# The opening and the first group put on a written time line, with wide exponentials and folds on two engines

## The chip, the cores and the metric

The kernel runs on one core of one Trainium2 chip. Its engines are TensorE (PE, matrix multiplications), VectorE (DVE), ScalarE (ACT), GpSimd (POOL) and SyncE (SP, which issues most DMA transfers). Each works through its own queue in order and waits on semaphores for the others; DMA transfers move data between the chip's memory (DRAM) and the on-chip memory (SBUF), and TensorE writes its results to accumulator banks (PSUM). The metric is the device time of one execution in microseconds (us), as the median of several runs. Profiles are of one execution each.

## The reference: what is computed

An attention block without the usual score matrix, followed by a Fourier mixing block. Input: `q`, `k`, `v` of shape (8 batches, 8 heads, 576 tokens, 64), and weights `w_ch1` (512 x 2048) and `w_ch2` (2048 x 512).

```python
q_s = softmax(q, axis=-1)            # over the 64 of a head
k_s = softmax(k, axis=2)             # over the 576 tokens
kv  = einsum('bhsd,bhse->bhde', k_s, v)
x   = einsum('bhsd,bhde->bhse', q_s, kv)   # then heads side by side: (8, 576, 512)
u   = x + real(fft(fft(x, axis=1), axis=2))
un  = (u - mean) / sqrt(var + 1e-6)  # over the 512
out = u + relu(un @ w_ch1) @ w_ch2
```

Both softmaxes subtract a maximum first and add 1e-9 to the sum.

## The kernel before

**Tiles and groups.** Tokens are rows of 128 partitions. A batch has four "own" tiles of 128 tokens, called by (c, u) with c and u in 0 and 1; the few tokens that these leave over are gathered for two batches at a time in one "shared" tile (rows 0, 32, 64 and 96 of it come from elsewhere in DRAM than the 31 rows after each). The eight batches and the shared rows make eight groups of 512 tokens that go through the two large matmuls: first "up" (with `w_ch1` and relu), then "down" (with `w_ch2`).

**Stages.** For a batch, the keys (four tiles of 128 x 576, two heads each) get a maximum, an exponential with its sum (L634), a transpose on TensorE (L652, L660), and the product with the values (L677); the result is scaled by the reciprocal (L689) into `kvr`. A query tile gets a maximum by head (L731), eight exponentials with one head each (L737), a sum and reciprocal (L742 to L744), a product with it (L750), a transpose (L758), and the product with `kvr` (L811). The Fourier transforms are done by folding: sums and differences of tiles and of mirrored columns (L866, L872, L881, L887, L888; all on VectorE for batch 0, divided between VectorE and GpSimd for later ones), then matmuls with tables (the "blocks", L922 and L925) and again (the "mixes", L959 and L962), whose results are added to x (L992, L993). The norm takes statistics (L1013), a root, and scales (L1034 for group 0), then transposes (L1048) into `unT` (L1056).

**The first group.** The weights come as 64-bit words and are converted block by block ("convert", L379 to L385: two operations on ScalarE, two on VectorE, an exact integer addition on GpSimd). Group 0 goes through plain matmuls with the converted blocks: L1122 (up, 16 steps of four matmuls) and L1131 (down, 64 matmuls). Meanwhile sums and differences of the weight blocks ("combine", L391 to L401) are made and stored to DRAM (L431 to L437), because the later groups use a Strassen scheme (L1186 and after). The attention of batch 1 is worked in between.

**What sets the order.** From the second group on, steps carry times and are sorted by them inside `tc.manual_schedule`: each engine's queue has exactly this order. The opening and the first group are outside it: their order on each engine follows a scheduler, which may exchange instructions, and small instructions that copy a value onto itself or combine two with an "and" of zero ("gates": L576, L290, L306, L310, L312) hold back what should come later. While batch 0's folds run, two pairs of junk matmuls (L234) keep TensorE busy.

The order of DMA issues is that of the queue which issues them. Transfers use eight completion semaphores in turn, and a transfer waits for the earlier user of its own. The shared tile of queries is loaded by ScalarE's queue in four pieces of 32 rows each, and a fifth transfer of 4 rows, from SyncE, then writes over the first row of each piece (`t_rows`, L330 and L331). The outputs of the same rows go out in pieces of 15 and 16 rows (`shared`).

## Time and profile before

| | |
|---|---|
| median of 3 runs | 1095.81 us (1094.34 to 1096.25) |
| the profiled execution | 1096.12 us |
| its span, first to last instruction | 1094.3 us |
| TensorE busy over the span | 1057.3 us (97%) |
| VectorE, ScalarE, GpSimd busy | 662.2, 413.8, 484.8 us |
| first matmul of group 0's up phase | 61.90 us from the span's start |
| first matmul of its down phase | 116.91 us |
| first matmul of the second group | 195.62 us |

How to read it: busy time on TensorE is an upper bound of its work, since matmuls overlap. A line of the timeline gives the start, the duration of the merged instructions, the engine, the line of the program, the operation, what it writes and reads, how many instructions are merged, and in brackets how long the engine sat idle before them and what released it. Because merged matmuls overlap with the next ones, the time from one start to the next is the better measure. In the chain that ended last, 82% of the span are TensorE's.

### The profile page before, as it was taken

The numbers are of one execution on the slowest core, as the hardware profiler recorded it, in microseconds if no ns is written. First come the engines' busy times: TensorE is split into PE (matmuls) and PEld (weight loads), VectorE is DVE, ScalarE is ACT, GpSimd is POOL, SyncE is SP. The second block draws the span as 40 slices with busy tenths as digits, with TensorE's granted clock in tenths as the row PEclk, the third lists the DMA queues.
The fourth block names the chain that finished last, engine by engine and source line by source line (L and its number), as shares of the span: only waits on it lengthen the run. The fifth ranks groups of instructions, "written<-read, shape, count | busy, mean of one in ns | idle before, by whom it ended". The sixth has DMA issues, their size and how long they took to land.

```text
span 1094.3 us, 16985 instructions
## 1 busy us (share of the span) xinstructions
PE 1057.3 (97%) x6336; PEld 918.2 (84%) x6336; DVE 662.2 (61%) x1304; ACT 413.8 (38%) x1001; POOL 484.8 (44%) x410
## 2 busy tenths in 40 slices
PE   5799989999999999999999999999999999999997
PEld 4644545888888899889998999889988998899896
DVE  6784796566545775757654775687547743562251
ACT  6685433552135314442344224521552132131200
POOL 1065572227323536255533742464435353554343
PEclk9999989999999999999999999999999999999999
DMA  9555787546997457555766576557644574576463
GB/s 306 189 199 187 268 283 243 171 146 217 315 325 260 175 192 261 193 187 193 245 233 209 175 246 208 206 201 243 236 164 155 197 254 165 204 243 213 168 242 124
DMA packets 114914, 236.42 MB, mean 216 GB/s; under 512 B 24320, under 2 KB 76288, under 8 KB 104208
## 3 DMA queue, kind: packets, MB, share of 16 engines
q1 hardware_dynamic: 113032, 234.29, 63.3%
q10 hardware_dynamic: 1800, 1.05, 0.3%
q8 instruction: 50, 0.82, 0.3%
q14 instruction: 32, 0.26, 0.1%
HBM read 200.18 MB, written 39.32 MB: 219 GB/s over the span
## 4 chain that ended last, share of the span: by engine, by line
PE 82%; DVE 3%; ACT 1%; issue 1%; POOL 1%; POOLq 0%; DVEq 0%; ACTq 0%
PE bb L1186 15%; PE bb L1312 10%; PE ba L1186 9%; PE bc L1186 9%; PE bc L1312 6%; PE ba L1312 6%; PE bb L1282 4%; PE acc L677 2%; PE acc L811 2%; PE bb L1397 2%; PE bc L1131 2%; PE acc L922 2%; PE acc L925 2%; PE acc L959 1%; PE bc L1397 1%; PE ba L1397 1%
## 5 line engine op out<-in xcount | busy, mean ns | idle before, releaser
L1186 PE MATMUL bb<-unT,big 128*128 128x256 f32 x768 | 184.1, 380 | 0.0
L391 POOL TENSOR_TENSOR big<-big 128x512 f32<-128x512 f32 (+1 forms) x38 | 46.3, 1219 | 278.6 <-ACT big L1198 277.8
L1186 PEld LDWEIGHTS bb<-unT,big 128*128 128x128 f32 x768 | 142.9, 190 | 18.8 <-DVE unT L1062 0.4
L1198 ACT ACTIVATE big<-big 128x512 f32<-128x512 f32 x96 | 60.4, 630 | 199.7 <-DVE big L1197 199.5
L1156 DVE TENSOR_TENSOR u<-bb,s 128x512 f32<-128x512 f32 x66 | 45.6, 691 | 130.2 <-PE bb L1186 114.3
L1186 PE MATMUL ba<-unT,big 128*128 128x256 f32 x512 | 123.9, 380 | 0.2 <-ACT unT L1056 0.2
L1186 PE MATMUL bc<-unT,big 128*128 128x256 f32 x512 | 123.9, 380 | 0.0
L1312 PE MATMUL bb<-big 128*128 128x128 f32 x848 | 105.2, 276 | 2.2 <-DVE u L1319 2.2
L1186 PEld LDWEIGHTS ba<-unT,big 128*128 128x128 f32 x512 | 94.7, 190 | 12.3 <-ACT unT L1056 0.5
L1186 PEld LDWEIGHTS bc<-unT,big 128*128 128x128 f32 x512 | 94.5, 190 | 12.1 <-DVE big L1197 0.9
L1312 PEld LDWEIGHTS bb<-big 128*128 128x128 f32 x848 | 99.7, 192 | 2.9 <-DVE u L1319 2.9
L1258 DVE TENSOR_TENSOR big<-big 128x512 f32<-128x512 f32 x92 | 83.0, 946 | 5.9 <-POOL big L392 3.4
L1262 POOL TENSOR_TENSOR x<-x,big 128x512 f32<-128x512 f32 x52 | 68.0, 1318 | 28.0 <-ACT big L1289 14.8
L1312 PE MATMUL ba<-big 128*128 128x128 f32 x640 | 79.6, 275 | 0.0
L1312 PEld LDWEIGHTS ba<-big 128*128 128x128 f32 x640 | 76.4, 192 | 1.2
L1258 POOL TENSOR_TENSOR big<-big 128x512 f32<-128x512 f32 x26 | 41.2, 1593 | 74.1 <-DVE big L1258 64.0
L737 ACT ACTIVATE q<-q,qm 128x64 f32<-128x64 f32 x240 | 64.6, 338 | 20.6 <-DVE qm L731 15.2
L1319 DVE TENSOR_TENSOR u<-bb,s 128x256 f32<-128x256 f32 x40 | 16.9, 423 | 70.5 <-PE bb L1312 61.8
L1282 PE MATMUL bb<-big 128*128 128x256 f32 x256 | 58.7, 381 | 0.0
L1197 DVE TENSOR_TENSOR big<-bc,u 128x512 f32<-128x512 f32 x64 | 44.0, 687 | 23.7 <-PE bc L1186 22.6
L1282 PEld LDWEIGHTS bb<-big 128*128 128x128 f32 x256 | 48.3, 190 | 7.9 <-DVE big L1197 1.1
L1312 PE MATMUL bc<-big 128*128 128x128 f32 x416 | 51.5, 275 | 0.0
(280 smaller groups left out, 2039.9 us busy)
## 6 DMA issues: line engine op xcount, KB each, us to landing
big<-w2d SPq DMA_DIRECT2D x67, 1024.0 KB, 4.9
big<-w1s SPq DMA_DIRECT2D x64, 896.0 KB, 4.9
big<-w2s SPq DMA_DIRECT2D x16, 1024.0 KB, 6.6
big<-in_w_dram SPq DMA_DIRECT2D x21, 512.0 KB, 5.9
w2d<-big SPq DMA_DIRECT2D x42, 256.0 KB, 6.1
q<-in_q_dram SPq DMA_DIRECT2D x27, 256.0 KB, 6.6
k<-in_kT_dram SPq DMA_DIRECT2D x24, 288.0 KB, 5.2
v<-in_v_dram SPq DMA_DIRECT2D x24, 256.0 KB, 5.2
```

Source lines behind the costliest of these rows:

```text
L391: e1.tensor_tensor(out=to(4), in0=at(2), in1=at(3), op=ALU.add)
L677: nc.tensor.matmul(pk, lhsT=ks[:, c, :], rhs=v[:, c, :], start=(c == 0), stop=(c == NC - 1))
L737: nc.scalar.activation(q[:, h, :], q[:, h, :], ACT.Exp, bias=m[:, h:h + 1])
L1156: plus = lambda t: V.tensor_tensor(out=temp(t), in0=box["bb"][:], in1=box["s1"][:], op=ALU.add)
L1186: nc.tensor.matmul(bank()[:, i, :], lhsT=w[:, WA_AT[m], k * P:(k + 1) * P], rhs=self.unT[g][:, B_AT[m], k, :], start=first and i == 0 and ...
L1197: steps = [(0, lambda: V.tensor_tensor(out=hp(i), in0=bank()[:], in1=u()[:], op=ALU.add)), (0.8, lambda: nc.scalar.activation(hp(i), hp(i) ...
L1198: (0.8, lambda: nc.scalar.activation(hp(i), hp(i), ACT.Relu))]
L1258: e.tensor_tensor(out=to(o), in0=to(x), in1=to(y), op=op)
L1262: G.tensor_tensor(out=x, in0=x, in1=tile(m), op=ALU.add)
L1282: nc.tensor.matmul(box[name][:, i, :], lhsT=h[p][:, A_AT[m], i * P:(i + 1) * P], rhs=self.stream[n][:, p, :], start=p == 0 and (m != 1 or ...
L1312: nc.tensor.matmul(box[place[n]][:, i, :], lhsT=own(m)(A_AT[n])[:, f, :], rhs=w[:, r // 2, r % 2 * P:r % 2 * P + P], start=first and f == ...
L1397: nc.tensor.matmul(bank()[:, i, :], lhsT=h[p][:, A_AT[m], i * P:(i + 1) * P], rhs=w[:, p, :], start=first and i == 0 and p == 0, stop=p == ...
```

## The change

The opening and the first group move into `tc.manual_schedule`. The opening's order is a table of step names with times (OPENING); a step is an operation of one engine or a few. In detail:

- Loads: the four key tiles of batch 0 are issued first, then values and queries in turn. The shared query rows come in four transfers of 31 rows and one of 4 rows, all on ScalarE's queue (`loads_first`).
- Queries of batch 0: GpSimd subtracts the maximum from the whole tile ("less"), and ScalarE takes one exponential of 512 columns ("exp"). For the own tiles the sum over a head comes from a matmul with a matrix of ones (`ones`) before the product with `kvr`, and its reciprocal scales the product.
- Keys of batches 0 and 1: the last 64 tokens of all four tiles are transposed together into `fifth`; the four products with the values share one bank, one reciprocal serves four tiles, and two operations of 64 x 4 x 64 scale.
- Folds of batch 0: the sums are GpSimd's, the differences VectorE's; GpSimd also takes the shared rows' folds and one of the two additions after each mix of batch 0.
- Norm of group 0: two of the four scalings are ScalarE's. The table of the root is loaded ahead ("roots").
- The junk matmuls and the gates are removed.
- Conversions and combinations are lists of timed steps. Combinations of the first layer come in the up phase, those of the second in the down phase (before, both came in the down phase). The attention of batch 1, its folds, mixes and norm get times in the group too.

```diff
+OPENING = """
+4.60 t max, 5.20 k00 max, 5.35 t less, 6.00 k00 exp, 6.20 k01 max, 6.76 t exp, 6.95 k00 turn, 7.20 k02 max,
+7.26 k01 exp, 7.87 t inverse, 8.02 k00 four, 8.21 k01 turn, 8.52 k02 exp, 8.72 k03 max, 9.28 k01 four,
...
+12.76 k00 kv, 13.09 B max, 13.59 t join, 13.69 A exp, 13.81 k01 kv, 14.29 B less, 14.71 A turn, 14.90 C max,
...
+23.56 k11 turn, 23.71 k10 four, 24.15 D out, 24.21 k11 four, 24.28 tokens0, 24.77 tokens2, 25.38 columns0,
+25.39 tokens3, 25.98 tokens1, 26.01 columns2, 26.37 columns3, 26.85 by3, 27.08 columns1, 27.20 c0 hi,
+27.21 by2, 27.69 again2, 27.85 c0 lo, 27.99 again3, 28.49 by0, 28.59 b2 times, 28.80 c1 hi, 28.85 by1,
...
+43.31 normal10, 43.67 normal11, 43.81 k1 scale1, 43.96 turn10, 44.22 laid00, 44.72 laid10, 44.87 turn11,
+45.62 laid11"""
...
-    def warm(self, t, n):
-
-        junk = self.turned()
-        for _ in range(n):
-            self.nc.tensor.matmul(junk[:, 0:2, :], lhsT=self.ident[:], rhs=t, start=True, stop=True)
...
-        last = self.t_rows(b, tail, nc.scalar)
-        t = self.small.tile([P, 1], F32, tag="root", name="root", bufs=1)
-        nc.scalar.activation(t[:], self.eps[:], ACT.Exp)
...
+        def shared():
+            flat = self.q.rearrange("b s n -> (b s) n")
+            for i in range(4):
+                a = i * S // 2 + P
+                nc.scalar.dma_start(tail[i * Q + 1:(i + 1) * Q], flat[a + 1:a + Q])
+            nc.scalar.dma_start(tail[0:P:Q], flat[0:2 * S:S // 2])
...
+        order = [shared, table, *(lambda r=r: keys(r) for r in range(NR)), lambda: values(0), lambda: queries(0),
+                 lambda: values(2), lambda: queries(1), self.tables, *(lambda r=r: second(r) for r in range(NR)),
+                 *(lambda i=i: fetch(i) for i in range(11))]
+        return [(i / 100, step) for i, step in enumerate(order)]
...
+        def last():
+            box["last"] = self.turned()
+            for r in range(NR):
+                nc.tensor.transpose(box["last"][:, r, :], ks[r][:, S - P:], self.ident[:])
+
+        def fifth():
+            copy(self.fifth[64:], box["last"][64:])
...
+        def scale(h):
+            s = slice(64 * h, 64 * h + 64)
+            V.tensor_tensor(out=self.kvr[b][s, :, s], in0=box["kv"][s, :, s],
+                            in1=rec[s].unsqueeze(2).to_broadcast([64, NR, 64]), op=ALU.mult)
...
+        def less():
+            m = live[it].pop()[:].unsqueeze(2).to_broadcast([P, H, DH])
+            nc.gpsimd.tensor_tensor(out=heads(), in0=heads(), in1=m, op=ALU.add)
+
+        def exp():
+            q = live[it][0]
+            nc.scalar.activation(q, q, ACT.Exp)
...
+            if b == 0:
+                n = {(0, 0): "bb", (1, 1): "bc", (0, 1): "ba", (1, 0): "bb"}[c, u]
+                t = self.ps.tile([P, 512], F32, tag=n, name=n)
+                box.append(t)
+                for r in range(NR):
+                    nc.tensor.matmul(t[:, 0:H], lhsT=qT[:, r, :], rhs=self.ones[:, r, :], start=r == 0, stop=r == NR - 1)
...
         def tokens_folded(some):
             for i in some:
-                e, op = ((V if b == 0 else G), ALU.add) if i < 2 else (V, ALU.subtract)
+                e, op = (G, ALU.add) if i < 2 else (V, ALU.subtract)
...
         def columns_folded(some):
             for i in some:
-                e, op = ((V if b == 0 else G), ALU.add) if i < 2 else (V, ALU.subtract)
+                e, op = (G, ALU.add) if i < 2 else (V, ALU.subtract)
                 t = eo[i]
                 e.tensor_tensor(out=t[:, 1:HD], in0=t[:, 1:HD], in1=t[:, D - 1:HD:-1], op=op)
-                if b == 0 and i > 1:
-                    self.warm(t[:, 0:HD], 2)
...
-            if self.turns == 2:
-
-                t = self.small.tile([P, 1], F32, tag="root", name="root", bufs=1)
-                nc.scalar.activation(t[:], sn[:, 0:1], ACT.Sqrt, scale=0.0)
...
+    first, second, both = 46.5, 56, 77
+    steps = blk.opening(fetch, converted)
+    up, down = blk.plain(0, lambda: blk.unT[0])
     for f in range(NF):
...
+        steps += at(first + 3.45 * f, up[f])
+    for i in range(2, 2 * NF - 6):
+        steps += at(first - 0.4 + 2 * (i - 2) if i < NF else first + 26 + 3 * (i - NF), converted(i))
+    for p, dt in enumerate((15, 20, 25, 35.5, 39, 42.5, 46, 50)):
+        steps += at(first + dt, combined(0, p))
+    t = first + second
+    for i, some in enumerate(down):
+        steps += at(t + 1.2 * i, some)
...
+    for p, dt in zip((3, 0, 1, 7, 2, 4, 5, 6), (28, 31, 34, 37, 46, 53, 58, 63)):
+        steps += at(t + dt, combined(1, p))
...
+        at_q = t - 14 + 6 * i
...
+        steps += at(at_q + 9, blk.q_turn(it)) + at(at_q + 13.5, blk.q_times_kv(it))
+    steps += at(t + 11, blk.t_times_kv(1)) + at(t + 19, blk.folded(1))
...
+    steps += at(t + 51, blk.norm(1)) + at(t, blk.ahead(2))
```

The names of the table: "t" is the shared query tile, "k02" key tile 2 of batch 0, A to D the own query tiles (0, 0), (1, 1), (0, 1), (1, 0), "tokens", "columns", "by" and "again" the four stages of the folds, "b2" a block, "m0" a mix, "c0" a conversion.

## The prediction

> **What bounds the kernel now.** I read the page's forty slices first, then the engines' busy time in stretches of 10 us, then the timeline of single engines where a stretch was thin. The slices:
>
> ```profile
> PE   5799989999999999999999999999999999999997
> PEclk9999989999999999999999999999999999999999
> ```
>
> TensorE is full from about 200 us on. What can be won lies in the first eight slices. From the built programs, the last 3018 matmuls, 989 VectorE and 365 SyncE instructions stand in one order in both kernels, so whatever moves the first matmul of the next group moves the end by the same amount. The timeline of TensorE gives the marks:
>
> ```profile
> 61.90 0.67 PE L1122 MATMUL ba<-unT,big 128*128 128x512 f32 x1 [1.12 <-ACT unT L1056]
> ...
> 143.07 2.08 PE L811 MATMUL acc<-kvr,qT 128*128 128x128 f32 x8 [4.01 <-ACT qT L768]
> 144.94 1.06 PE L758 MATMUL tr<-ident,spare 128*128 128x128 f32 x4
> 145.79 3.47 PE L1131 MATMUL ba<-big 128*128 128x512 f32 x4
> ...
> 195.62 1.99 PE L1186 MATMUL ba<-unT,big 128*128 128x256 f32 x8 [0.24 <-ACT unT L1056]
> ```
>
> The opening lasts 61.90 us, the first group 133.72 us. In the group TensorE idles 4.01 us, and then L811 takes 1.87 us from start to start where it takes 0.89 elsewhere, L758 0.85 for 0.44, four L1131 3.31 for 1.72: 2.98 us more at a low clock. With the 0.24 before L1186 that is 7.2 us; the other 126.5 are work. The low clock is in the stretches too:
>
> ```profile
> 130.00:140.00 10.00, 9.06 (x39) 5.13 (x37) 7.92 (x18) 3.33 (x8) 7.03 (x9) 1.00 0.75 293
> 140.00:150.00 10.00, 6.93 (x19) 4.50 (x20) 9.97 (x13) 6.36 (x12) 7.21 (x7) 0.66 0.68 247
> ```
>
> (window, TensorE, its weight loads, VectorE, ScalarE, GpSimd, then the clock.) How the opening begins, on VectorE, then on the two DMA queues:
>
> ```profile
> 4.13 0.75 DVE L628 TENSOR_REDUCE km<-big 128x1 f32<-128x576 f32 x1 [4.13 <-DMA big<-in_kT_dram]
> ...
> 7.87 0.75 DVE L628 TENSOR_REDUCE km<-big 128x1 f32<-128x576 f32 x1 [1.91 <-DMA big<-in_kT_dram]
> ```
>
> ```profile
> 0.75 1.90 ACTq L330 DMA_DIRECT2D big<-in_q_dram  x4
> ```
>
> ```profile
> 7.55 0.69 SPq L331 DMA_DIRECT2D big<-in_q_dram  x1
> ```
>
> The DMA view of the first 30 us has ScalarE's queue and the rates:
>
> ```profile
> GB/s 0 0 110 270 340 296 329 304 303 350 369 352 178 256 306 311 330 284 374 370 387 391 389 365 359 344 326 331 332 333 330 306 339 345 352 350 350 347 350 348
> ...
> q10 hardware_dynamic: 192, 0.26, 3.0%
> ```
>
> VectorE starts when key tile 0 lands, 3.4 us after its issue. The four loads of 32 shared query rows are all in by 7.55, where L331, which writes over them, is let go. Their 192 packets are 4 x (32 rows + 16).
>
> **What the skill says.** In "DMA: Bandwidth & Descriptors", section "Why a DMA increments its semaphore by 16 and not by 1", the Trainium skill says that a transfer is split over the largest count of engines, up to 16, that divides its outermost size, and gives 127 partitions as an example of one engine, the lowest. The 16 packets beside each 32 rows agree with 16 engines; no transfer of a prime count of rows is in this trace. "SBUF — State Buffer", section "Who interferes with whom", says that a VectorE instruction with two SBUF inputs and a GpSimd one that reads SBUF hold the shared ports in turn. This trace agrees:
>
> ```profile
> 156.04 3.12 POOL L866 TENSOR_TENSOR eo<-x 128x512 f32<-128x512 f32 x2
> ```
>
> ```profile
> 156.28 1.75 DVE L866 TENSOR_TENSOR eo<-x 128x512 f32<-128x512 f32 x1
> 157.96 1.35 DVE L849 TENSOR_TENSOR eo<-eo 128x128 f32<-128x128 f32 x1
> ```
>
> Alone the same VectorE instructions take 0.68 (at 154.26) and 0.29 (at 26.97). "TensorE: Matmul & The Clock Gate", section "Part 1: The HAM clock gate", halves the clock after an idle window of about 3.4 us; the 4.01 above, with 6 us of doubled times after it, agrees.
>
> **The change, part by part.** The new names are those of the table OPENING.
>
> *The shared query load.* Four loads of 32 rows, overwritten by a fifth, become four of 31 and a fifth of 4 rows, all from ScalarE; the fifth waits until the first has landed. "t max", which needs all five, is now VectorE's first instruction: the key maxima, then every exponential, wait behind it. 31 is prime. If the rule holds, 4 x 31 x 2048 B = 254 KB go through one engine, which also carries a sixteenth of what SyncE has under way: four key tiles (73.7 KB), the first values (41.0), the first queries (32.8). That is 401 KB. A sixteenth of 350 to 389 GB/s is 21.9 to 24.3 GB/s, so 16.5 to 18.3 us. Key tile 0 shows what lies around moving: 3.4 us less its 18.4 KB (0.84) = 2.55. Issued at 0.75, the rows land at 19.8 to 21.6; I take 20.5. Ends: 13.8 if the queue were served first (254 KB at 24.3 = 10.5), 23.5 if the second values come between. SyncE suffers as well: its loads wait for semaphores in turn with those loads, so values and queries come late; the second queries, near 25, are needed only at about 31. If the rows spread as before, they land near 8.4: 7.55, and the fifth after that.
>
> *From that landing (L) to the first up matmul.* Five rows of the sum:
> - "t max" 0.60 and key maximum 0 0.70; ScalarE then has four key exponentials (0.78), a wide one for t (about 0.6, from 0.68 for 576 columns) and copies (0.5); the last transposes at the cold 1.05, and the copy "k0 fifth" 0.55: first keys-times-values at L + 8.7.
> - Four of these at 1.22 and a turn at 0.44, two scales of 0.45, "t kv" 0.9 and hand-overs: L + 16.0. One shared reciprocal and two scales stand for four and eight (0.29 each). Of the own tiles' 8 x 0.25 us of exponentials, one of 0.6 each remains; ScalarE isn't what this stretch waits for.
> - Four own tiles: 0.89 each, and the new head sums by matmul: eight passes of 8 columns. No row shows such a pass. Below, nothing; above, 0.86 by the skill's weight-load price (page above, "LDWEIGHTS": 107 ns for 128 columns). I take 0.7. With a turn: 6.8, L + 22.8.
> - The folds. VectorE alone took from 32.47 to 38.35 for the part the sine blocks need. Divided, GpSimd's 1.25 + 0.65 + 1.25 + 0.65 alternate with VectorE's 0.53 + 0.53 + 0.27 + 0.27 (0.08 to 0.15 of each is not port time), 5.4, and then by3, by2, again2 and again3 take 1.5; with the last product's copy 7.2: L + 30.0. Below, about 5 if the ports didn't clash.
> - TensorE has nothing for about 6 us of that (L234's warming matmuls are removed), so the five blocks cost 4.9 + 3.0 at the low clock (0 to 3.5), copies 0.7: first mix at L + 38.6. Mix to up took 61.90 - 46.99 = 14.9; 1.3 of it goes with L973's table load (1.28), now earlier, 1.1 with two of four scalings moved to ScalarE: 12.5. Up at L + 51.1.
>
> With 20.5 this is 71.6, 9.7 us later than now.
>
> *Weights and group 0.* Conversions are the same work, one each 2 to 3 us. The first layer's combinations move into the up phase, where GpSimd was free from 103 to 114 us: 8 x 1.44 us there beside 24 additions of 1.25, 42 of TensorE's 55. Their stores pass the fetches of later weights on SyncE, and a combination that overwrites a stored block waits for the landing (4.8 us in the DMA table), with VectorE's and GpSimd's conversions queued behind it: some 4 us, three times, which the 13 free ones hide. Without that cover up would wait for a conversion, but these run a dozen us ahead. Gates (L576, L290, L310, L306) go. So the 4.01 + 2.98 of before go, in which ScalarE stood behind L576 and combinations. I leave 2.5 us (0 to 7) for new waits: the first query turn has 1.6 us of room behind VectorE. Group: 129.0, 4.7 less. Loads for the next groups are only reordered, under a full TensorE: nothing.
>
> Sum: +9.7 - 4.7 = +5.0. Span 1099.3; the profiled execution's 1096.12 becomes 1101.1, and the median of the runs lies 0.3 below it: about 1100.5.
>
> **The rivals.**
> *Spread after all* (the other side). The loads use all engines, L = 8.4: up at 59.5, 2.4 earlier, and the group's 4.7: 1089. For it: 16 engines at 32 rows, and OPENING sets "t max" at 4.60. Against: the code loads 32 rows and overwrites one elsewhere, and splits the same 31 rows in 15 + 16 for the output. It decides where L is below 61.9 + 4.7 - 51.1 = 15.5.
> *Half late.* One engine, but its rows get more than an even share, or the folds and the clock cost their lower ends: L near 15, or 66 for up: 1096, no change.
> *The plan as written.* Up at 46.5, 15.4 earlier, with the group 20: 1076. Against: it needs ports that don't clash and rows at 4.60.
> *Group 0 stalls.* VectorE, held behind a combination that waits for stores, delays the first query turn; 4 us idle and 3 of low clock come back: 1108.
>
> **How the numbers follow.** Main case 0.62 (1094 to 1107), spread 0.15, half late 0.15, plan 0.03, stall 0.05. The landing's ends alone give -7 to +3, the unknown prices -6 to +1. The range 1086 to 1108 leaves out the plan, half of spread's lower part and the worst. Within 0.2% (2.2 us) is about what a measurement can't tell from none. Slower: 0.54 of the main case, stall, 0.02 of half late, 0.61. Same: 0.14. Faster: spread, plan, and the rest, 0.25.
>
> **What would show it.** ScalarE's queue: 128 rows + 4 x 1 + 4 = 136 packets if narrow, 208 if spread. VectorE's first instruction near 20.5, released by a DMA; the DMA rate below 200 GB/s before it. Folds with doubled VectorE times; blocks near 1.9 us; up near 71.6; group 0 at 129. The prediction falls if "t max" starts before 15.

## The result, and the profile after

The changed kernel takes 1119.78 us (median; 1118.97 to 1120.43), the kernel before, on the same chip, 1095.07: a ratio of 1.0225, 95% interval 1.0208 to 1.0243. The forecast was 1100.5 and its range ended at 1108. The sign was right, the size was not: 24.7 us where 5 were forecast.

The profiled execution of the changed kernel took 1118.97 us, its span 1117.2, against 1096.12 and 1094.3 before. The two marks on TensorE's timeline divide the difference of 22.9:

| stretch | before | forecast | after |
|---|---|---|---|
| opening, to the first up product | 61.90 | 71.6 | 70.93 |
| group 0, to the second group's first product | 133.72 | 129.0 | 147.82 |
| second group's first product at | 195.62 | 200.6 | 218.75 |

The opening came out 0.7 us from the forecast. Group 0 was to gain 4.7 us and lost 14.1: the whole miss is there.

The opening first. VectorE's first instruction, in VectorE's timeline (start, duration, operation; in brackets the idle time before it and what ended it):

```profile
19.82 0.69 DVE L798 TENSOR_REDUCE qm<-big 128x8 f32<-128x512 f32 x1 [19.82 <-DMA big<-in_q_dram]
```

And the DMA view of the first 30 us, the rates in forty equal slices, then ScalarE's queue:

```profile
GB/s 0 0 150 248 325 358 370 120 51 250 389 75 26 26 25 23 27 190 179 384 167 25 111 371 385 53 25 52 150 418 437 395 391 404 342 387 357 371 378 351
...
q10 hardware_dynamic: 136, 0.26, 2.3%
```

136 packets is the count forecast for one engine a load. The stretches at 23 to 27 GB/s are that one engine, with nothing else under way: SyncE's queue waits for these rows before it issues the next values and queries (5.9, 3.0 and 3.1 us; the first of these waits covers 9 to 11.8 us). Before, the same forty slices fall under 170 GB/s only at the very start. The sign "below 200 GB/s before it" came only in part: 17 of the 26 slices before 19.5 us are below.

Now group 0, in TensorE's timeline:

```profile
70.93 5.37 PE L1156 MATMUL ba<-unT,big 128*128 128x512 f32 x8 [0.77 <-ACT unT L1110]
...
129.94 1.09 PE L815 MATMUL tr<-ident,q 128*128 128x128 f32 x4 [5.58 <-DVE q L787]
...
173.66 1.82 PE L994 MATMUL acc<-ft,eo 128*128 128x144 f32 x4 [6.36 <-DVE eo L963]
```

(With a gap in the records of a few tenths, the idle times before these two are 5.75 and 6.5 us.) Added up against the 126.5 us of work that the prediction found: 1.8 us of low clock at the first up product (5.20 us to the next line, where 3.43 is usual); 5.75 idle before the first query turn and 1.5 of low clock behind it; 2.7 idle before the next turns and a product; 6.5 idle before batch 1's first block and 2.1 of low clock; 1.0 at the norm's turns. That is 21.3, and 126.5 + 21.3 is the 147.8 measured. Both long waits end on VectorE. How full it is, in stretches of 10 us (window, TensorE, its weight loads, VectorE, ScalarE, GpSimd, clock, DMA share, rate):

```profile
120.00:130.00 10.00, 4.42 (x12) 1.71 (x11) 9.65 (x15) 5.19 (x14) 6.80 (x7) 0.97 0.93 335
...
170.00:180.00 10.00, 6.19 (x21) 4.23 (x22) 9.03 (x16) 1.10 (x6) 7.30 (x10) 0.66 0.56 183
```

TensorE waits where VectorE is full. Before that VectorE isn't full: from 100 to 120 us it is busy 14.7 of 20, and stands 2.11 and 1.55 us for additions of GpSimd (up to 109.08 and 112.05). A third line, from VectorE's timeline, is where VectorE itself stood still, 30 us earlier, behind a combination whose result tile was still being stored:

```profile
98.36 0.43 DVE L419 TENSOR_TENSOR s<-u,big 128x256 f32<-128x256 f32 x1 [4.05 <-DMA w1s<-s]
```

From the second group on the two kernels' instructions stand in one order, and the 23.1 us by which it starts later are the 22.9 of the spans.

### The profile page after: what moved, and what is told of

The parts are those of the page before. It is cut to its first block, busy times and chain, and to the rows that moved or that the text cites. A ratio compares the mean times of both kernels' runs of the same rounds, so it can differ in the third digit from the quotient of the medians.

```text
span 1117.2 us, 16942 instructions
## 1 busy us (share of the span) xinstructions
PE 1058.9 (95%) x6360; PEld 919.0 (82%) x6360; DVE 657.9 (59%) x1240; ACT 403.6 (36%) x956; POOL 498.2 (45%) x422
## 4 chain that ended last, share of the span: by engine, by line
PE 79%; DVE 5%; ACT 2%; POOL 1%; issue 1%; DVEq 0%; ACTq 0%; POOLq 0%
PE bb L1230 14%; PE bb L1356 9%; PE bc L1230 9%; PE ba L1230 9%; PE bc L1356 6%; PE ba L1356 6%; PE bb L1326 4%; PE acc L706 2%; PE acc L875 2%; PE bb L1441 2%; PE acc L994 2%; PE acc L997 2%; PE acc L1022 1%; PE bc L1441 1%; PE ba L1441 1%; PE tr L1102 1%
## 5 line engine op out<-in xcount | busy, mean ns | idle before, releaser
L375 POOL TENSOR_TENSOR big<-big 128x512 f32<-128x512 f32 x32 | 40.9, 1277 | 284.0 <-ACT big L1242 284.0
L1302 POOL TENSOR_TENSOR big<-big 128x512 f32<-128x512 f32 x26 | 40.9, 1582 | 74.4 <-DVE big L1302 64.0
```

The source lines that it names most:

```text
L375: e1.tensor_tensor(out=to(4), in0=at(2), in1=at(3), op=ALU.add)
L1302: e.tensor_tensor(out=to(o), in0=to(x), in1=to(y), op=op)
```

## The experiments

Where nothing else is said, each is the changed kernel with one edit; "up" is the start of the first up product, "group" the time from there to the second group's first product. The kernel before took 1094.5 to 1095.7 us on the chips that shared these runs.

| run | us | ratio to before, 95% | up | group |
|---|---|---|---|---|
| changed kernel | 1119.78 | 1.0225 (1.0208 to 1.0243) | 70.93 | 147.8 |
| 1 loads of 32 rows | 1113.13 | 1.0162 (1.0140 to 1.0184) | 64.95 | 150.1 |
| 2 before, with 31 rows | 1107.38 | 1.0109 (1.0094 to 1.0124) | 75.51 | 132.7 |
| 3 combinations late | 1121.24 | 1.0240 (1.0223 to 1.0258) | 70.86 | 150.3 |
| 4 folds clear | 1111.54 | 1.0146 (1.0130 to 1.0163) | 71.71 | 140.9 |
| 5 own result tile | 1118.18 | 1.0201 (1.0184 to 1.0217) | 72.15 | 147.7 |
| 6 queries early | 1117.76 | 1.0210 (1.0195 to 1.0224) | 70.08 | 147.0 |
| 7 folds on VectorE | 1119.44 | 1.0216 (1.0201 to 1.0231) | 69.19 | 149.5 |
| 8 five edits | 1101.92 | 1.0060 (1.0047 to 1.0073) | 62.02 | 139.9 |
| 9 VectorE's part small | 1118.87 | 1.0212 (1.0198 to 1.0225) | 70.64 | 146.7 |
| 10 seven edits | 1092.09 | 0.9979 (0.9967 to 0.9990) | 60.77 | 132.3 |
| 11 warming matmuls | 1117.48 | 1.0209 (1.0190 to 1.0229) | 70.77 | 145.7 |
| 12 both parts small | 1114.78 | 1.0171 (1.0157 to 1.0185) | 70.49 | 143.3 |
| 13 conversions apart | 1117.66 | 1.0200 (1.0185 to 1.0215) | 72.05 | 148.0 |
| 14 eight edits | 1094.46 | 1.0006 (0.9989 to 1.0023) | 60.93 | 132.5 |
| 15 nine edits | 1091.89 | 0.9967 (0.9955 to 0.9979) | 59.34 | 132.7 |

The executions of one kernel lie 1.5 to 4.6 us apart in the changed kernel and runs 1 to 9 and 11 to 13. The medians of runs 3, 5, 6, 7, 9, 11 and 13 are within 2.3 us of the changed kernel's and their intervals overlap with its own, so no gain or loss in time is shown for any of them alone; for these the traces have to speak. They scatter too: in the eight kernels that share the changed kernel's opening (it and runs 3, 4, 5, 6, 9, 12 and 13) "up" lies from 70.08 to 72.15, and from the landing of the shared tile to "up" it is 50.4 to 52.6 us.

### The opening: the shape of the load

Run 1 puts the 32-row shape back:

```diff
-                nc.scalar.dma_start(tail[i * Q + 1:(i + 1) * Q], flat[a + 1:a + Q])
+                nc.scalar.dma_start(tail[i * Q:(i + 1) * Q], flat[a:a + Q])
```

> The changed kernel with the shared query tile's four loads of 32 rows again, in place of 31 (the strided load of the four head rows comes after them and overwrites row 0 of each). Theory that the 31-row shape sets the opening: VectorE's first instruction starts near 8 us in place of 19.8, ScalarE's queue shows about 192 to 208 packets in place of 136, the up products start at 59 to 61 us in place of 70.9, the time is 1108 (1106 to 1110). Rival, that the keys and values or the chain behind them would set it all the same: up at 66 or later, time over 1114.

Run 2 puts the 31-row shape, alone, into the kernel before (`o` is 1 on ScalarE's queue and 0 elsewhere):

```diff
-            e.dma_start(q[i * Q:(i + 1) * Q], flat[at:at + Q])
+            o = int(e is self.nc.scalar)
+            e.dma_start(q[i * Q + o:(i + 1) * Q], flat[at + o:at + Q])
```

> The kernel before with one thing changed: its four loads of the shared queries on ScalarE's queue take 31 rows and not 32. Theory that the shape costs by itself, through one DMA engine's 25 GB/s and through the loads that queue behind it: the shared tile's maximum, at 10.6 us before, comes at 19 to 21, the up products start 5 to 10 us later than 61.9, time 1100 to 1105. Rival, that the old order, with the keys ahead of the shared queries on VectorE, hides the late tile: up within 2 us of 61.9, time under 1097.5.

Run 2 took 12.1 us more than the kernel before, by one changed line, above what either theory had. Its VectorE timeline, after that of the kernel before:

```profile
8.63 0.75 DVE L628 TENSOR_REDUCE km<-big 128x1 f32<-128x576 f32 x1
...
10.62 0.69 DVE L731 TENSOR_REDUCE qm<-big 128x8 f32<-128x512 f32 x1
```

```profile
5.53 0.75 DVE L629 TENSOR_REDUCE km<-big 128x1 f32<-128x576 f32 x1 [5.53 <-DMA big<-in_kT_dram]
19.21 0.69 DVE L732 TENSOR_REDUCE qm<-big 128x8 f32<-128x512 f32 x1 [12.93 <-DMA big<-in_q_dram]
```

One key tile is ahead of the shared tile there, and the rest of VectorE's queue stands behind it for 12.93 us; the up products start 13.6 us late. But this isn't the old order. The opening of the kernel before is left to the scheduler, and with 31 rows it placed the shared tile's maximum after one key maximum and not after three (the third is the line at 8.63). SyncE's order of issues changed too: the load of the four head rows has nothing to overwrite now and goes out at 2.24 in place of 7.55, and key tiles 1 and 2, which wait for the narrow loads, at 6.75 in place of 2.21, tile 3 at 15.16 in place of 8.72. So the 12.1 us are the price of the one line with all that follows from it in this program; the time contradicts the rival, but whether an order with the keys ahead would hide the late tile wasn't tested.

In run 1 ScalarE's queue has 200 packets, and the up products start 6.0 us sooner; group 0 gave 2.3 of that back, with the same waits. Time and "up" lie between what theory and rival said. The tile landed at 12.30 us and not near 8:

```profile
12.30 0.69 DVE L798 TENSOR_REDUCE qm<-big 128x8 f32<-128x512 f32 x1 [12.30 <-DMA big<-in_q_dram]
```

The fifth load, which overwrites one row of each of the four others, is issued only at 7.40, when they are in, and behind values and queries that SyncE issued from 4.07 on. (In run 14 below it is issued at 6.96 ahead of these, and the tile's maximum starts at 9.03.) The theory holds for the cause; the size expected, 11.5 us, took the landing for 4 us earlier than it was.

### Batch 1's folds

Run 4 takes everything else out of VectorE's and GpSimd's queues among these folds:

```diff
-    for i, dt in zip(range(2 * NF - 6, 2 * NF), (0, 13, 15.5, 18, 20.5, 23)):
+    for i, dt in zip(range(2 * NF - 6, 2 * NF), (0, 13, 33, 35.5, 38, 40.5)):
...
-    for p, dt in zip((3, 0, 1, 7, 2, 4, 5, 6), (28, 31, 34, 37, 46, 53, 58, 63)):
+    for p, dt in zip((3, 0, 1, 7, 2, 4, 5, 6), (34, 37, 40, 46, 50, 55, 60, 65)):
```

> The changed kernel with the last four conversions moved from 15.5 to 23 us after the first down product's place to 33 to 40.5, and the second layer's combinations 3 to 9 us later, so that nothing else stands in VectorE's and GpSimd's queues among batch 1's folds. Theory that these make the folds late: the wait of 6.4 us at the first block falls to under 1 and the 2.1 us of low clock behind it go: 1111 to 1113. Rival, that the folds are late because the last own product is late, or that the down products then wait for the late weights: over 1117.

8.2 us less, as the theory had it; the group is 6.9 us shorter, after 1.2 us came back as a longer wait at the norm's turns (1.55 for 0.33). In the changed kernel VectorE's folds of batch 1 run from 159.04 us, and between them stand two conversions and a combination:

```profile
159.04 3.44 DVE L943 TENSOR_TENSOR eo<-x 128x512 f32<-128x512 f32 x2
163.66 0.43 DVE L361 TENSOR_SCALAR big<-spare 128x512 int32<-128x512 int32 x1 [1.18 <-POOL big L369]
164.12 0.69 DVE L364 SCALAR_TENSOR_TENSOR big<-spare,big 128x512 int32<-128x512 int32 x1
...
169.70 0.94 DVE L419 TENSOR_TENSOR spare<-big 128x256 f32<-128x256 f32 x1
170.68 1.38 DVE L419 TENSOR_TENSOR spare<-big,spare 128x256 f32<-128x256 f32 x1
```

With them out of the way the block no longer waits; TensorE's timeline of run 4 shows it with neither idle time nor a doubled duration (0.66 for 1.82):

```profile
168.43 0.66 PE L994 MATMUL acc<-ft,eo 128*128 128x144 f32 x4
```

The down products did not wait for the later weights either. So the 6.5 + 2.1 us were a matter of order in VectorE's and GpSimd's queues. Which of the two it was, the run doesn't tell, since the moved steps use both.

### The first query turn

There are several theories on why VectorE is late there.

Run 3, the first layer's combinations in the down products, where the kernel before had them, with three loads for the second group moved behind them:

```diff
-    for p, dt in enumerate((15, 20, 25, 35.5, 39, 42.5, 46, 50)):
+    for p, dt in enumerate((48, 51.6, 55.2, 58.8, 62.4, 66, 69.6, 73.2)):
...
-    steps += [(t + 4 + 2 * i, lambda i=i: blk.load(i)) for i in range(3)]
+    steps += [(t + 22 + 2 * i, lambda i=i: blk.load(i)) for i in range(3)]
```

> The changed kernel with the eight combinations of the first layer's weights moved from the up products to the down products (from 15 to 50 us after the first up product's place to 48 to 73), and the three loads of the second group behind them. Theory that these combinations, with their waits for stores and their clash with GpSimd, make VectorE late for the first query turn: the idle 5.75 us and the low clock of 1.5 at that turn go, and the 2.7 us at the next turns, so 8 to 10 us less: 1110 to 1112, unless the combinations now delay batch 1's folds, which would show as a longer wait than 6.4 us at its first block. Rival, that the conversions alone make VectorE late or that the turn's slot is too early: over 1117.

1121.24: over the rival's bound, and yet the first turn's wait did go (at 124.13 it has none). It came back at the later turns, as 1.4, 0.9 and, at the fourth, 4.5 us, and VectorE's timeline says why:

```profile
147.88 0.88 DVE L419 TENSOR_TENSOR big<-big 128x256 f32<-128x256 f32 x2 [6.24 <-DMA w1s<-big]
```

A combination stands 6.24 us for a store, and the fourth tile's sums stand behind it. The combinations are part of the cause, and moving them only moves the place.

Run 5 gives the second combination a result tile of its own, so that it waits for no store:

```diff
-            t, four = [temp("s1"), temp("u2")] if p == 0 else [temp("u3"), temp("s1")], None
+            t, four = [temp("s1"), temp("u2")] if p == 0 else [temp("u3"), pairs(self.halves()[:, 0:D])], None
```

> The changed kernel with one buffer changed: the second combination of the first layer's weights writes one of its two results into a tile of its own, and not into the one that the first combination's store still has to read. VectorE stands idle 4.05 us at 98.4 us for that store. Theory that this wait is the root of the late first query turn (nothing is made up later, VectorE being full from there): the wait goes and the idle time before the first query turn falls from 5.75 to 1.7 to 3 us, with the low clock behind it: 1114 to 1116. Rival, that VectorE's later waits on GpSimd and on the next stores take the same time up again: 1118 to 1120.

The wait of 4.05 us went; the turn's fell from 5.58 to 4.52, the time by 1.6 us (about the spread of these runs), the group by nothing. The rival holds: most of a single wait is taken up again on the way. At 109.45 and 112.42 VectorE still stands 2.11 and 1.55 us for GpSimd, as without the edit; the expectation had VectorE full from there, and it wasn't.

Run 6 moves the first three query tiles' VectorE and ScalarE work 8 us forward:

```diff
-        steps += at(t - 34 + i if i < 3 else t + 0.6, blk.q_load(it)) + at(at_q, blk.q_exp(it))
+        steps += at(t - 34 + i if i < 3 else t + 0.6, blk.q_load(it)) + at(at_q - 8 * (i < 3), blk.q_exp(it))
```

> The changed kernel with the maximum, exponentials and inverses of batch 1's first three own query tiles placed 8 us earlier, their turns on TensorE left where they are. Theory that the queries' place in VectorE's order, behind conversions and combinations that run late, makes the turn wait: the idle 5.75 us and the 1.5 us of low clock go, the smaller waits of 2.7 us at the next turns partly: 1111 to 1114. Rival, that the work moved ahead delays the conversions by as much, so that down products or batch 1's folds are late in its place: over 1117.

The turn no longer waits, but the medians differ by 2.0 us and the groups by 0.8, not by 6. In its TensorE timeline the idle time stands in two other places, both now behind ScalarE:

```profile
123.89 5.37 PE L1156 MATMUL bc<-unT,big 128*128 128x512 f32 x8 [3.29 <-ACT big L1161]
...
136.03 1.16 PE L875 MATMUL acc<-kvr,qT 128*128 128x128 f32 x8 [2.90 <-ACT qT L825]
```

The exponentials now stand ahead of an up product's eviction (L1161) and of a turn's copy (L825) in ScalarE's queue, and wait there for maxima that VectorE still makes late. Neither theory had this; the rival's number holds.

Run 9 asks whether it is the amount of VectorE's work. Six of the eight combinations have VectorE's two differences cut to 2 columns; the kernel leaves out the other 254:

```diff
-            e.tensor_tensor(out=place(o), in0=x, in1=y, op=how)
+            n = 2 if layer == 0 and p > 1 and e is nc.vector else HD
+            e.tensor_tensor(out=place(o)[:, 0:n], in0=x[:, 0:n], in1=y[:, 0:n], op=how)
```

> The changed kernel with VectorE's part of the first-layer combinations cut: for six of the eight, its two differences are made on 2 columns in place of 256, the rest of them is left out; GpSimd's part, the stores and every place in the order stay. That takes some 10 us of VectorE's time (12 instructions of 0.43 to 1.2 us) out of the 65 us from the first up product to the last own query tile. Theory that VectorE is simply behind with its work by then, so that whatever stands in its queue makes the first query turn wait: the idle 5.75 us and its 1.5 us of low clock go, and most of the 2.7 us at the next turns: 1109 to 1112. Rival, that the waits for stores and for GpSimd's part hold the queue, not the amount of work: over 1117.

The theory fell: the median is 0.9 us lower, the wait 3.72 for 5.58. The groups of VectorE instructions by form, from 98 to 140 us of run 9, show what it had missed (count, busy us, mean ns, and the idle time before them); first the same twelve in the changed kernel:

```profile
L419 DVE TENSOR_TENSOR big<-big 128x256 f32<-128x256 f32 x12 | 11.9, 989 | 1.7 <-POOL big L419 1.2
```

```profile
L420 DVE TENSOR_TENSOR big<-big 128x2 f32<-128x2 f32 x12 | 7.8, 652 | 3.4 <-DMA w1s<-big 1.6 <-POOL big L420 1.2
...
L420 DVE TENSOR_TENSOR s<-u,big 128x256 f32<-128x256 f32 x1 | 0.4, 426 | 4.1 <-DMA w1s<-s 4.1
```

A difference of 2 columns takes 652 ns on average, where one of 256 columns takes 426 with GpSimd idle. So the edit took 4.1 us out of VectorE's queue and not the 10 expected, and 1.7 of these came back as idle time; as a test of the amount of work it is weaker than it was meant to be. One such pair in VectorE's timeline, and GpSimd's beside it:

```profile
114.95 1.91 DVE L420 TENSOR_TENSOR big<-big 128x2 f32<-128x2 f32 x2 [0.86 <-POOL big L420]
```

```profile
114.19 1.41 POOL L420 TENSOR_TENSOR big<-big 128x256 f32<-128x256 f32 x2
115.56 1.28 POOL L369 TENSOR_TENSOR big<-big,words 128x512 int32<-128x512 int32 x1
```

The pair ends with GpSimd's instruction, at 116.86 and 116.84. The Trainium skill ("SBUF — State Buffer", section "Who interferes with whom") calls the shared ports "an exclusive lock", held for a whole instruction, and says that issue order, not shape, decides who blocks; this run agrees: GpSimd's addition keeps its 1.28 us, and 2 columns of VectorE end with it. (The 0.86 us in front of the pair is another matter: both differences need GpSimd's first sum.) VectorE's share of a combination costs what GpSimd happens to be doing more than its own columns.

Run 12 cuts GpSimd's part as well (the condition on the engine goes), and leaves out 254 columns there too:

> The changed kernel with six of the eight first-layer combinations cut on both engines: all four sums and differences of each are made on 2 columns in place of 256, the rest is left out; stores and places in the order stay. With VectorE's part alone cut, VectorE's two instructions still took up to 1.9 us a pair, as long as GpSimd's beside them, and the idle time before the first query turn went from 5.75 to 3.72 us only. Theory that GpSimd's part, which VectorE's instruction has to sit out, is the larger share: the idle time falls below 1.5 us and the next turns' with it: 1109 to 1114. Rival, that the waits for stores, which stay, are the larger share: idle still over 3 us, time over 1116.

The wait fell to 1.12 us, the group by 4.6, the time by 5.0, just short of the theory's 1109 to 1114; of TensorE's 7.8 us idle before 155 us, 3.2 are left. VectorE's part of these 4.7 us of idle time was 1.3 (run 9), GpSimd's part the other 3.4. The next turns' waits hardly changed. Ahead of what is left at the first turn stands a store, in TensorE's timeline and in VectorE's, where the query's sums come next:

```profile
125.04 0.63 PE L816 MATMUL tr<-ident,q 128*128 128x128 f32 x4 [1.12 <-DMA w1s<-big]
```

```profile
122.67 0.36 DVE L420 TENSOR_TENSOR big<-big 128x2 f32<-128x2 f32 x2 [2.06 <-DMA w1s<-big]
```

Run 13 spaces the conversions:

```diff
-        steps += at(first - 0.4 + 2 * (i - 2) if i < NF else first + 26 + 3 * (i - NF), converted(i))
+        steps += at(first - 0.4 + 2 * (i - 2) if i < NF else first + 26 + 3.7 * (i - NF), converted(i))
...
-    for i, dt in zip(range(2 * NF - 6, 2 * NF), (0, 13, 15.5, 18, 20.5, 23)):
+    for i, dt in zip(range(2 * NF - 6, 2 * NF), (7, 14, 15.5, 18, 20.5, 23)):
```

> The changed kernel with the first ten conversions of the second layer's weights 3.7 us apart in place of 3 (and the next two at 7 and 14 us after the first down product's place in place of 0 and 13). Nothing is left out. Theory that the conversions which need VectorE, ScalarE and GpSimd in turn are as much in the way as the combinations: with one or two fewer of them ahead of each query step the first turn waits 3 us or less in place of 5.75 and the following turns next to nothing: 1113 to 1116. Rival, that the combinations alone hold the queue up: 1118 or more.

The first turn waits 4.62, the group is what it was: alone, the edit is worth nothing in the profile, which is of the slowest of four executions (2.1 us in the medians). The rival is nearer, though its number was a little high.

### The divided folds and the removed warming

Run 7 has batch 0's folds on VectorE alone (this line, and its like in the fold of the columns):

```diff
-                e, op = (G, ALU.add) if i < 2 else (V, ALU.subtract)
+                e, op = (G if b else V, ALU.add) if i < 2 else (V, ALU.subtract)
```

> The changed kernel with batch 0's folds all on VectorE, as they are not divided any more between VectorE and GpSimd. Theory of the prediction, that the two engines hold each other up so that dividing gains little: the first two steps of the folds take 4 x 0.69 + 4 x 0.42 = 4.4 us on VectorE alone in place of 5.2 from 43.2 to 48.5 us in the divided form, so the first block starts within 1 us of where it did, and the time is 1119 to 1121. Rival, that the division is worth what it says, half of the folds' time: 2.5 us or more slower, over 1122.

The first block starts 29.55 us after the shared tile's landing, against 30.2 in the changed kernel (29.9 to 30.4 in the eight that share its opening), and the time is the same (1119.44). Divided, VectorE's first two pairs take 2.38 and 2.35 us; alone on VectorE a pair of the first kind takes 1.28. Dividing these folds gains nothing.

Run 11 gives TensorE something to do during them:

```diff
+    def warm(self, t, n):
...
                 e.tensor_tensor(out=t[:, 1:HD], in0=t[:, 1:HD], in1=t[:, D - 1:HD:-1], op=op)
+                if b == 0:
+                    self.warm(t[:, 0:HD], 3)
```

> The changed kernel with one addition: 12 matmuls of 256 columns into an unused bank on TensorE while batch 0 is folded, as the kernel before has 8. Theory that TensorE's idle 6 us set its clock back: the ten blocks, 1.17 us each until 54.4 us, take 0.65 us each from the start, the up products start 2 to 2.6 us sooner, the time is 1117 to 1118. Rival, that VectorE's chain of sums and norms sets the start of the up products whatever the blocks take: 1119 or more.

All ten blocks take 0.65 us, but 12 matmuls are too many: they end only at 52.1, where the first block then starts. (The kernel before has four, 8 records in its trace: the expectation's 8 counts records, its 12 matmuls.) Counted from the landing (20.17), the up products start after 50.6 us, within the scatter of the others; the first of them now runs at full clock (3.67 for 5.37). The median is 2.3 us lower, of the size expected, but it isn't clear of the spread, and what the trace shows of it is at the first up product and not at the blocks. What the blocks lost to the low clock is 2.2 us in the changed kernel (7.13 us from the first to the end of the tenth, 4.89 here); most of it was not regained here.

### The edits together

Run 8: runs 1, 4, 5 and 6, and in the table OPENING the shared tile's nine steps 4.4 us later, so that "k00 max" heads VectorE's queue.

> The changed kernel with five edits at once: 32-row loads of the shared queries; the keys' maxima ahead of the shared queries' on VectorE, whose steps up to their turn come 4.4 us later; the late conversions and second-layer combinations behind batch 1's folds; the own tile for the second combination's result; batch 1's first three queries 8 us earlier. If the waits are separate, as the theory has it: 6.7 and 8.2 us measured for the first and third, 3 or 4 from the keys, 7 for the queries: 1119.8 - 25 = 1095, level with the kernel before or a little faster (1092 to 1098). Rival, that the waits stand in for each other, one coming up where another is taken away: over 1102.

1101.92 is the rival's bound to within 0.1. Yet the four edits tried alone add up to 18.5 us and the five together gave 17.9: apart from the key order, put at 3 or 4 and never tried alone, they nearly added. What the sum of 25 had wrong most of all was 7 us for the queries, where run 6 gave 2.0. The opening is back at 62.02 and the folds' wait is gone, but the two waits behind ScalarE that run 6 had brought up are still 2.61 and 4.59 us.

Run 10 adds runs 11 and 13:

> The five edits of the last combined kernel and two more: the first ten conversions of the second layer's weights 3.7 us apart in place of 3, so that four of them fall among the down products, where VectorE stands idle for 8 us, and 12 short matmuls on TensorE during batch 0's folds. Theory of VectorE's backlog: the two waits that are left at the query turns (2.6 and 4.6 us) fall to under 2 together, the blocks run at full clock and save 2.6: 1092 to 1096, the kernel before or a little better. Rival, that the waits come from ScalarE's queue, whose copies stand behind the exponentials, and come up again: 1099 or more.

9.8 us less (8.9 by the ratios to the kernel before), though alone the two had been worth about 2 each. The first ScalarE wait is gone, and the second is 1.5:

```profile
119.81 1.16 PE L881 MATMUL acc<-kvr,qT 128*128 128x128 f32 x8 [1.53 <-ACT qT L831]
```

The group takes 132.3 us, 7.6 less than in run 8. The idle time before 155 us fell by 5.7, the rest is low clock. The two were not tried apart in this kernel; the warming ends some 70 us before these waits and "up" moved by 1.25 us, so the spacing is the likelier for the group. That is argued, not shown.

Run 14 moves the strided load from ScalarE's queue to SyncE's, behind the keys, since ScalarE issues it at 6.93 and every exponential stands behind it:

```diff
-            nc.scalar.dma_start(tail[0:P:Q], flat[0:2 * S:S // 2])
+        def heads():
...
+            load(tail[0:P:Q], flat[0:2 * S:S // 2])
```

> The last combined kernel with one more edit: the strided load of the four head rows goes to SyncE's queue behind the keys, and not to ScalarE's, where the table load and so every exponential stood behind its issue until 8.1 us. Theory that ScalarE is then the first to be late: its first exponential starts near 5 us in place of 9.5, the first kv product 3 to 5 us sooner, the up products at 56 to 59 in place of 60.8: 1088 to 1090. Rival, that the shared tile's maximum (12.9 us) sets the opening: within 1 us of 1092.1.

The first exponential starts at 4.67 us and the shared tile's maximum at 9.03, and the up products not a moment sooner (60.93); the spans of the two profiles are 1091.4 and 1091.1. The median is 2.4 us above run 10's, but the executions lie from 1092.92 to 1101.01, five of the fourteen above 1099.9; the profile is of one of the other nine, and what sets the five apart stays open. The theory fell, and not for the rival's reason, since the shared tile's maximum came early as well. The next late thing, in VectorE's timeline, is the load of the first own query tile, and behind it stand the keys' fifth-chunk copy and the shared tile's sums:

```profile
14.68 0.69 DVE L807 TENSOR_REDUCE qm<-big 128x8 f32<-128x512 f32 x1 [4.65 <-DMA big<-in_q_dram]
15.40 0.69 DVE L549 COPY big<-tr 64x512 f32<-64x512 f32 x1
16.12 0.69 DVE L785 TENSOR_REDUCE qrec<-big 128x8 f32<-128x512 f32 x1
```

Run 15 puts that maximum behind them ("A max" at 12.25 for 11.40, "t inverse" and "t normal" at 12.06 and 12.10, and "t turn", "t copy", "t fold", "t join" about 1.8 us earlier):

> The last combined kernel with VectorE's order changed in the opening: the maximum of the first own query tile, which waits for its load until 14.7 us, comes after the fifth-chunk copy of the keys and after the shared tile's inverse and normalization, and the shared tile's turn, copy and fold come 1.8 us earlier. Theory that the late own tile at the head of VectorE's queue kept the early keys from paying: the copy comes near 12 us in place of 15.4, the first kv product is done by 13, the shared product comes 2 us or more sooner than 24.9, the up products before 59.5 in place of 60.9: 1089 to 1092. Rival, that the load of the own tiles itself sets the opening, whatever stands behind it: up within 1 us of 60.9, 1093 or more.

The copy now starts at 10.79, the shared product at 22.90 in place of 24.93, the up products at 59.34. 1091.89 us, a ratio of 0.9967 (0.9955 to 0.9979) to the kernel before: 2.6 us faster, and 27.9 faster than the change as it was made. It is 0.2 us below run 10, whose interval overlaps: "up" came 1.4 us earlier than there, but in the time the last two edits show nothing. Of the parts of the change, these nine edits leave the shared reciprocals, the wide exponentials, the explicit time line and the divided folds in place.

## Why the prediction was right or wrong

**The shared query load: right.** L was 19.82 for 20.5 (19.8 to 21.6), 136 packets as computed for one engine, the rate 23 to 27 GB/s where 21.9 to 24.3 were worked out. Run 1 shows the cause: with 32 rows the tile is there at 12.30.

**From the landing to the first up product: right within 1 us at every mark.** First keys-times-values at L + 8.05 for 8.7, "t kv" done at L + 15.6 for 16.0, head sums 0.81 us each (start of one pass group to the product after it, 35.40 to 36.21) for 0.7, the last own product's end at L + 23.2 for 22.8, folds 7.0 for 7.2, first block at L + 30.2 for 30.0, low clock 2.2 for 3.0, first mix at L + 37.75 for 38.6, mix to up 13.4 for 12.5, up at L + 51.1 for 51.1. That the last agrees to the tenth is luck: the errors before and after the first mix, 0.85 and 0.9, cancel, and kernels with the same opening lie 2 us apart there. The port clash that the sum of the folds rests on is borne out by VectorE's pairs (2.38 us divided, 1.28 alone) and by run 7: without the division the folds are not slower. One slip at the end: 1101.1 less 0.3 is 1100.8, not 1100.5.

**"Group 0: 129.0": wrong, and the step that failed is "I leave 2.5 us (0 to 7) for new waits".** It measured 21.3. The reasoning behind it failed in three places.

- "Some 4 us, three times, which the 13 free ones hide." The first such wait is there, 4.05 us at 98.36. But the 13 free us were GpSimd's (55 of the up phase less its 42 of work), and the wait fell on VectorE, from 94.3 to 98.4. Room was counted on the wrong engine. It wasn't the largest term, though: run 5, without this wait, is 1.6 us lower. The larger term was that a combination holds VectorE for as long as GpSimd's part takes (run 12, 5.0 us; run 9, with VectorE's part alone cut, 0.9). The prediction knew the clash, and priced it for the folds; for the eight combinations it priced GpSimd's 1.44 us and nothing for VectorE.
- "These run a dozen us ahead." The conversions do; no up product waits for one. But the queries and the folds stand in the same queue, and have no such lead. The one sentence on them, "the first query turn has 1.6 us of room behind VectorE", gave the place of the largest wait, and the price was not carried on from it: the first query's maximum, placed 42 us after the first up product's place, started 50.7 us after it, at 121.63.
- Batch 1's folds were not priced at all. The conversions and combinations placed among them, on engines that hold each other up, cost 6.5 us and 2.1 of low clock: 8.2 in run 4, the largest single edit.

The expected gain, 4.01 + 2.98 us of before, did come: the longest wait for ScalarE's copy is now 1.19 us, at 143.11, without a low clock behind it. The same kind of wait came up at two other places, each long enough to bring the low clock with it.

**The rival "Group 0 stalls" was nearest to the true case.** It named the queue and the first place, and its 7 us are what that place cost (5.75 idle and 1.5 of low clock). Of the reason that it gave, a combination that waits for stores, run 5 shows a small part only. It had one stall, 1108, where there were two large ones and several small ones, and a chance of 0.05. "Spread after all" and "half late" are refuted by the packets and L.

**Expectations that fell on the way.** That VectorE's amount of work makes the turn late (run 9). That one wait for a store is its root (run 5). That the waits are separate and add up: runs 1, 4, 5 and 6 did so nearly, with 6.7, 8.2, 1.6 and 2.0 us alone and 17.9 together with the new key order; but the spacing and the warming, 2.1 and 2.3 alone, gave 9.8. What remains open is a division of the first turns' 7 to 10 us into causes that add: of the 7.8 us of idle time, 4.7 go with the combinations' running time on both engines (run 12) and 1.3 with one store's wait (run 5), each as the only edit; the rest was not taken apart.

## What to carry to other kernels

When work is moved under a busy engine, price it in the queue of every engine that it shares with something urgent, at the time at which it lands there: idle time on one engine in another stretch hides nothing. An instruction that shares ports with another engine costs what that engine is doing as well: 254 of 256 columns cut saved a third of its time (989 to 652 ns, run 9). And an in-order queue gives a wait back at the next urgent instruction behind it, so what an edit gives alone can be far from what it gives in a set (4.4 us for two edits, 9.8 on top of five others), and an early instruction whose data come late is worse than a late one.

## What the runs showed of the hardware

- One line, 31 rows in place of 32 in four loads, cost 12.1 us of 1095 (run 2, with the changes of order that followed from it). With nothing else under way these rows move at 23 to 27 GB/s.
- A VectorE difference of 2 columns took 652 ns on average beside GpSimd, and 426 for 256 columns without it; the same differences with 256 columns took 989 beside GpSimd.
- After 3.29 us of idle time on TensorE eight up matmuls took 5.21 us from start to start for the usual 3.43 (run 6, at 123.89); after 3.72 us and one turn they took 3.70 (run 9, at 128.26). In these two the length of the idle time alone didn't decide about the clock.
- Eight passes of 8 columns in f32 take 0.81 us, about 0.1 each.
- A strided load of four rows, issued at 7.40 us behind values and queries, landed at 12.30 (run 1); issued at 6.96 ahead of them, it was in by 9.03 (run 14).
